# Decode-attention backward, 32 heads on one core: the second half of one head's dV stored as 124 and 4 partitions

## The chip, the cores and the metric

The kernel runs on one core of one Trainium2 chip. The core has five engines: TensorE for matrix products (PE; its weight loads are listed apart as PEld), VectorE (DVE), ScalarE (ACT), GpSimd (POOL) and SyncE (SP), which here only issues transfers. Besides them 16 DMA engines move data between the chip's memory (DRAM in the names) and the on-chip buffer SBUF, which has 128 partitions. A DMA instruction is issued by one engine's queue; it is cut into packets, each DMA engine moves its share in the order of issue, and each leaves a mark on a semaphore when its share has landed. The metric is device time in microseconds, from the program's start to its end; smaller is better.

## The reference

The reference runs softmax attention for 32 heads with one query row per head and 8192 keys of width 128 in bf16, and then its gradients for a given grad_out:

```
scores = einsum('bhqd,bhkd->bhqk', q, k) * scale
attn   = softmax(scores)
out    = einsum('bhqk,bhkd->bhqd', attn, v)
# and the vector-Jacobian product: dq, dk, dv
```

With p the attention row of a head and dO its grad_out row: dV = p (outer) dO, dP = V dO, dS = p * (dP - p.dP) * scale, dK = dS (outer) q and dQ = dS K. For each head two tensors of 2 MB are read (K, V) and two of 2 MB are written (dK, dV): 134.23 MB in and 134.23 MB out over the 32 heads.

## The kernel before

One loop over heads h from 0 to 32 (line 255 on) works on two heads at a time: the scores and dV of head h, and dK and dQ of head h - 1. The order of instructions on each engine is the order in which the code is written; the loop is a schedule made by hand.

A head's tensor lies in SBUF as 128 partitions of 64 rows of 128 values, so partition p holds rows 64p to 64p + 63, which is 16 KB that are contiguous in DRAM too. `load_k` (line 74) and `load_v` (line 78) issue one DMA of 2 MB each for a head; K has three buffers, V two. The gradients are made by `outer(h, which, r)` on VectorE: each call multiplies a quarter of the rows (r = 0 to 3; 128 x 2048 values, line 210) into a buffer `G_dk` or `G_dv`. Each of the two has two buffers, so head h needs the buffer that head h - 2 stored from.

`outer` also issues the store. Normally there is one DMA of 2 MB after r = 3 (`parts = 1`). For the first and the last head the store is cut in two halves along the rows of each partition (`parts = 2`): rows 0 to 31 of every partition after r = 1, rows 32 to 63 after r = 3. Each half has 128 partitions of 8 KB. All loads of K and V and all stores are issued on SP, in program order, and all of them go into one queue (q1). Towards the end that order is: load of V of head 31, dV of head 29, dK of head 29, dV of head 30, dK of head 30, dV of head 31 in two halves, the output row `out_0`, dK of head 31 in two halves, dQ. There are no loads after V of head 31. The small results `out_0` and dQ are 32 partitions of 256 bytes (line 253).

The semaphores that tell of landings are handed out in turn from eight, and a DMA waits until the one that used its semaphore last has landed. The dV of head 30 is stored from a buffer which no later head uses.

Of the kernel before, what the change touches and what calls it, by code (L numbers as in the profile page):

```python
# [23 lines left out]
def kernel(  # L24
# [11 lines left out]
    nc = tc.nc  # L36
    P = 128
    _, H, S, D = k.shape
# [23 lines left out]
    def rows_of(x, h, c, parts):  # L62
        L = NT // parts
        return x[0, h].rearrange("(p n) d -> p n d", p=P)[:, c * L:(c + 1) * L, :]

    def slots(X, c, parts):
        L = NT // parts
        return X[:, c * L:(c + 1) * L, :]
# [134 lines left out]
    def outer(h, which, r):  # L203
        x = st[h]
        if r == 0:
            x[which] = gpool.tile([P, NT, D], BF16, tag=which, name="G_" + which)
        G, dst = x[which], out_2 if which == "dk" else out_3
        rep, row = x["ds"] if which == "dk" else x["p"], x["qd"][:, 0 if which == "dk" else 1, :]
        Q = NT // 4
        nc.vector.tensor_tensor(  # L210
            slots(G, r, 4).rearrange("p n (a b) -> p n a b", b=R),
            slots(rep, r, 4).unsqueeze(2).to_broadcast([P, Q, D // R, R]),
            row.rearrange("p (a b) -> p a b", b=R).unsqueeze(1).to_broadcast([P, Q, D // R, R]),
            op=ALU.mult)
        parts = 1
        if h == 0 or h == H - 1:
            parts = 2
        if r % (4 // parts) == 4 // parts - 1:
            c = r // (4 // parts)
            nc.sync.dma_start(rows_of(dst, h, c, parts), slots(G, c, parts))  # L220

    def rows_bc(h):
        x = st[h]
# [31 lines left out]
    for h in range(H + 1):  # L255
# [9 lines left out]
        if h > 0:  # L265
            ds_of(p_)
            outer(p_, "dk", 0)
            dq_of(p_, 0)
# [3 lines left out]
        if h > 0:  # L272
            dq_of(p_, 1)
            outer(p_, "dk", 1)
# [9 lines left out]
        if h > 0:  # L284
            outer(p_, "dk", 2)
# [75 lines left out]
```

## Time and profile before

| what | value |
|---|---|
| median of 4 runs | 646.18 us (645.99 to 646.27) |
| the profiled execution | 646.26 us, of which 644.3 us span |
| DVE busy | 505.3 us (78%) |
| PE busy | 480.7 us (75%) |
| ACT busy | 183.6 us (28%) |
| moved by DMA | 269.80 MB, mean 419 GB/s over the span |
| mean granted TensorE clock | 0.599 |

The span goes from the first to the last instruction of the core; what lies around it in the profiled execution is 2.0 us. A busy share is an engine's own time at work. The strip of slices cuts the span in 40 equal parts of 16.1 us; its DMA row is the mean over the 16 DMA engines, in tenths, so that 8 can mean that all work for eight tenths of the time or that some have stopped. The queue table counts packets by queue: q1 carries what SP issues, q10 what ACT issues, and q8 and q14 fetch the engines' instructions. In the listing of instructions in order of time SPq stands for SP's sequencer: the moment a DMA is issued, not when it moves. In the table of waits each row is "who waited, for whom: us in total, times, longest". In the table of stretches the DMA share is again the mean over 16 engines, and 1.00 or a little more means that none of them rests.

### The profile page before, as it was taken

How to read it: one execution, taken by the hardware profiler on the slowest of the kernel's cores; microseconds unless marked ns; L12 is line 12 of the kernel's file. 1: busy time of each engine (PE TensorE's matmuls, PEld its weight loads, DVE VectorE, ACT ScalarE, POOL GpSimd, SP SyncE). 2: the span in 40 equal slices, each digit the busy share in tenths (PEclk: the TensorE clock that was granted, in tenths of full speed). 3: DMA queues.
4: the chain of work that ended last, by engine and by line, in shares of the span. 5: the costliest groups of instructions: out<-in, count | busy, mean ns of one | idle time of the engine just before them, and what ended most of it. 6: DMA issues, size and time to landing. Idle time of an engine off the chain costs nothing.

```text
span 644.3 us, 20935 instructions
## 1 busy us (share of the span) xinstructions
PE 480.7 (75%) x9673; PEld 451.7 (70%) x9673; DVE 505.3 (78%) x653; ACT 183.6 (28%) x332; POOL 0.7 (0%) x6
## 2 busy tenths in 40 slices
PE   2898888887677867778767787667786777877770
PEld 2888778886677866768666777667785676866670
DVE  5999898877977779777788777797767977778860
ACT  2333333232233221233222332223322223231230
POOL 0000000000000000000000000000000000000000
PEclk9666666665666655666656665556665666655665
DMA  8999999999999999999999999999999999999985
GB/s 349 405 426 429 426 421 430 425 428 429 427 429 426 428 428 425 432 424 431 427 426 429 427 428 429 427 426 425 430 426 426 427 429 427 427 430 426 428 367 241
DMA packets 19718, 269.80 MB, mean 419 GB/s; under 512 B 2352, under 2 KB 2352, under 8 KB 2864
## 3 DMA queue, kind: packets, MB, share of 16 engines
q1 hardware_dynamic: 19584, 268.47, 98.2%
q8 instruction: 75, 1.23, 0.7%
q14 instruction: 11, 0.09, 0.0%
q10 hardware_dynamic: 48, 0.01, 0.0%
HBM read 134.23 MB, written 134.23 MB: 417 GB/s over the span
## 4 chain that ended last, share of the span: by engine, by line
DMA 59%; PE 21%; DVE 14%; ACT 2%; issue 1%; SPq 0%; DVEq 0%; ACTq 0%
DMA Kt<-in_k_dram 48%; DVE XK_sb L146 8%; PE T_ps L183 8%; DMA out_dram<-G_dv 5%; DMA out_dram<-G_dk 5%; PE s_ps L157 5%; DVE G_dk L210 4%; PE dp_ps L200 3%; PE m_ps L200 2%; PE dp_ps L195 2%; ACT XT_sb L185 1%; PE m_ps L294 1%; DVE G_dv L210 1%; PE s_ps L173 1%; DVE sm L163 1%
## 5 line engine op out<-in xcount | busy, mean ns | idle before, releaser
L210 DVE TENSOR_TENSOR G_dv<-p_rep,qd 128x2048 bf16<-128x2048 bf16 x128 | 148.2, 1219 | 89.5 <-DMA out_dram<-G_dv 83.8
L183 PE MATMUL T_ps<-ident_f,Vt 128*128 128x128 f32 x1024 | 203.1, 382 | 0.2 <-PE m_ps L294 0.2
L183 PEld LDWEIGHTS T_ps<-ident_f,Vt 128*128 128x128 f32 x1024 | 190.5, 210 | 0.3 <-issue 0.2
L185 ACT COPY XT_sb<-T_ps 128x1024 f32<-128x1024 f32 x128 | 128.7, 1013 | 129.0 <-PE T_ps L183 126.9
L210 DVE TENSOR_TENSOR G_dk<-ds_rep,qd 128x2048 bf16<-128x2048 bf16 x128 | 155.6, 1218 | 2.4 <-DMA out_dram<-G_dk 1.4
L146 DVE STREAM_TRANSPOSE XK_sb<-Kt 128x1024 f32<-128x1024 f32 x128 | 148.2, 1213 | 5.9 <-DMA Kt<-in_k_dram 5.2
L157 PEld LDWEIGHTS <-XK_sb 128*128 128x128 bf16 x2048 | 57.6, 104 | 90.8 <-DVE pdt L234 79.8
L157 PE MATMUL s_ps<-q_blk,XK_sb 128*128 128x4 bf16 x2048 | 59.7, 168 | 82.2 <-DVE pdt L234 72.1
L195 PE MATMUL dp_ps<-do_blk,XT_sb 128*128 128x2 bf16 x2048 | 66.8, 164 | 17.9 <-ACT XT_sb L185 17.9
L195 PEld LDWEIGHTS <-XT_sb 128*128 128x128 bf16 x2048 | 65.1, 103 | 20.5 <-ACT XT_sb L185 20.5
L200 PE MATMUL dp_ps<-ds_rep,Kt 128*128 128x1 bf16 x2048 | 64.1, 165 | 1.6 <-issue 1.3
L200 PEld LDWEIGHTS <-Kt 128*128 128x128 bf16 x2048 | 59.6, 104 | 6.9 <-issue 6.8
L244 ACT COPY dq_all<-dp_ps 128x1 f32<-128x1 f32 x32 | 5.1, 159 | 192.3 <-PE dp_ps L200 185.4
L200 PEld LDWEIGHTS <-Vt 128*128 128x128 bf16 x2048 | 57.6, 97 | 1.0
L200 PE MATMUL m_ps<-p_rep,Vt 128*128 128x1 bf16 x2048 | 56.8, 164 | 0.0
L294 PEld LDWEIGHTS m_ps<-rs,ones_f 128*128 128x128 f32 x64 | 16.0, 311 | 49.9 <-ACT e L293 49.9
L294 PE MATMUL m_ps<-rs,ones_f 128*128 128x1 f32 x64 | 18.8, 362 | 40.5 <-ACT e L293 40.5
L303 ACT ACTIVATE p_rep<-e,rinv 128x256 bf16<-128x256 f32 x32 | 16.3, 509 | 30.0 <-DVE rinv L301 30.0
L163 DVE TENSOR_TENSOR sm<-s_ps,in_quad 128x256 f32<-128x256 f32 x32 | 13.6, 424 | 11.3 <-PE s_ps L157 8.2
L229 ACT CAST qd<-s_ps 128x256 bf16<-128x256 f32 x32 | 11.9, 372 | 32.2 <-PE s_ps L225 32.2
L236 DVE SCALAR_TENSOR_TENSOR ds_rep<-dp_ps,pdt,p_s 128x256 bf16<-128x256 f32 x32 | 15.5, 484 | 5.5 <-PE dp_ps L195 2.5
L293 ACT ACTIVATE e<-s_ps,nbias 128x64 f32<-128x64 f32 x32 | 10.0, 313 | 31.6 <-DVE nbias L290 31.6
(44 smaller groups left out, 143.3 us busy)
## 6 DMA issues: line engine op xcount, KB each, us to landing
Vt<-in_v_dram SPq DMA_DIRECT2D x32, 2048.0 KB, 30.0
Kt<-in_k_dram SPq DMA_DIRECT2D x31, 2048.0 KB, 30.8
out_dram<-G_dv SPq DMA_DIRECT2D x30, 2048.0 KB, 34.5
out_dram<-G_dk SPq DMA_DIRECT2D x30, 2048.0 KB, 33.6
out_dram<-G_dv SPq DMA_DIRECT2D x4, 1024.0 KB, 15.1
out_dram<-G_dk SPq DMA_DIRECT2D x4, 1024.0 KB, 13.5
Kt<-in_k_dram SPq DMA_DIRECT2D x4, 512.0 KB, 5.2
out_dram<-fin_sb SPq DMA_DIRECT2D x2, 8.0 KB, 13.4
```

Source lines behind the costliest of these rows:

```text
L146: nc.vector.transpose(XK[h][:, :, :, u, :], slots(Kt[h], u, NCH).rearrange("p g d -> p (g d)").bitcast(F32).rearrange("p (g w j) -> p g w ...
L157: nc.tensor.matmul(out[:, g, :], lhsT=cols[:, g, c // 2, c % 2], rhs=q_blk[:, h, c, :], start=(c == 0), stop=(c == 2 * NB - 1), skip_group ...
L163: nc.vector.tensor_tensor(x["sm"][:], x["s"][:, 0:NT].rearrange("p (a g) -> p a g", a=NQ).unsqueeze(2) .to_broadcast([P, NQ, NCH, CH]), in ...
L183: nc.tensor.transpose(T_ps[:, i, :], words[:, m * P:(m + 1) * P], ident_f[:])
L185: nc.scalar.copy(X[:], T_ps[:])
L195: nc.tensor.matmul(st[h]["dp"][:, n:n + 2], lhsT=X[:, i, e2, :], rhs=do_blk[:, h, e2, :], start=(e2 == 0), stop=(e2 == 1), skip_group_chec ...
L200: nc.tensor.matmul(out_col, lhsT=Xt[:, n, :], rhs=rep[:, n, 0:1], start=(n == 0), stop=(n == NT - 1), skip_group_check=True)
L210: nc.vector.tensor_tensor(slots(G, r, 4).rearrange("p n (a b) -> p n a b", b=R), slots(rep, r, 4).unsqueeze(2).to_broadcast([P, Q, D // R, ...
L229: nc.scalar.copy(x["qd"][:].rearrange("p a d -> p (a d)"), x["s"][:, 256:512])
L236: nc.vector.scalar_tensor_tensor(out=x["ds"][:], in0=x["dp"][:, 0:NT].unsqueeze(2).to_broadcast([P, NT, R]), scalar=pdt[:], in1=x["p_s"][: ...
L294: nc.tensor.matmul(x["m"][:, 0:1], lhsT=ones_f[:], rhs=rs[:], start=True, stop=True, skip_group_check=True)
L303: nc.scalar.activation(x["p"][:], e[:].unsqueeze(2).to_broadcast([P, NT, R]), ACT.Copy, scale=rinv[:])
```

## The change

For dV of head 30 (H - 2) the store is now cut in two halves as for the first and the last head. The first half goes out after r = 1 as 128 partitions. The second half goes out after r = 3 as two DMAs: partitions 0 to 123, and partitions 124 to 127. The bytes stored, their place in DRAM and all computation are the same; dK of head 30 is still one store.

```diff
         parts = 1
-        if h == 0 or h == H - 1:
+        if h == 0 or h == H - 1 or (h == H - 2 and which == "dv"):
             parts = 2
         if r % (4 // parts) == 4 // parts - 1:
             c = r // (4 // parts)
-            nc.sync.dma_start(rows_of(dst, h, c, parts), slots(G, c, parts))
+            if h == H - 2 and c == 1:
+
+                for lo, hi in ((0, P - 4), (P - 4, P)):
+                    nc.sync.dma_start(rows_of(dst, h, c, parts)[lo:hi], slots(G, c, parts)[lo:hi])
+            else:
+                nc.sync.dma_start(rows_of(dst, h, c, parts), slots(G, c, parts))
```

Described in a few words, the change is: second half of dV of head 30 stored as 124 and 4 partitions, so that these 1 MB move on DMA engines 0 to 3 alone.

## The prediction

> **What bounds the kernel now.** I read the strip of slices first, then the queues, then the stretches of the tail, the sync engine's issues, its waits, and last the single completion marks.
>
> ```profile
> span 644.3 us, 20935 instructions
> ...
> DMA  8999999999999999999999999999999999999985
> GB/s 349 405 426 429 426 421 430 425 428 429 427 429 426 428 428 425 432 424 431 427 426 429 427 428 429 427 426 425 430 426 426 427 429 427 427 430 426 428 367 241
> ...
> q1 hardware_dynamic: 19584, 268.47, 98.2%
> q8 instruction: 75, 1.23, 0.7%
> q14 instruction: 11, 0.09, 0.0%
> ```
>
> No compute engine is above 78% busy; the 16 DMA engines are at nine tenths or more from the second slice to the 38th, at about 428 GB/s. Transfers set the pace. Only the last two slices (8 and 5 tenths) have room. The second line to keep is q8: 75 packets that are no data of the kernel, but its instructions.
>
> ```profile
> core 0: us, PE busy (x) PEld busy (x) DVE busy (x) ACT busy (x) POOL busy (x), PEclk, DMA share, GB/s
> 560.00:600.00 40.00, 30.95 (x612) 29.16 (x610) 32.16 (x41) 11.31 (x21) 0.00 (x0) 0.57 1.01 428
> 600.00:610.00 10.00, 6.43 (x189) 5.96 (x185) 9.02 (x12) 1.54 (x3) 0.00 (x0) 0.60 1.02 431
> 610.00:620.00 10.00, 8.53 (x107) 7.92 (x108) 6.11 (x11) 3.91 (x7) 0.00 (x0) 0.54 0.89 377
> 620.00:630.00 10.00, 5.96 (x170) 5.50 (x167) 8.06 (x9) 2.37 (x8) 0.00 (x0) 0.63 0.90 377
> 630.00:633.00 3.00, 0.00 (x0) 0.00 (x0) 0.00 (x0) 0.00 (x0) 0.00 (x0) 0.50 0.96 404
> 633.00:640.00 7.00, 0.00 (x0) 0.00 (x0) 0.00 (x0) 0.00 (x0) 0.00 (x0) 0.50 0.57 240
> 640.00:643.00 3.00, 0.00 (x0) 0.00 (x0) 0.00 (x0) 0.00 (x0) 0.00 (x0) 0.50 0.18 72
> ```
>
> The DMA share falls to 0.57 and stays there for seven microseconds: 0.57 x 16 is nine engines at work and seven with nothing left. All computing has ended by 630.
>
> ```profile
> start us, us, engine line op out<-in xcount [idle before <-releaser]
> 593.76 0.33 SPq L220 DMA_DIRECT2D out_dram<-G_dk  x1
> 602.40 0.33 SPq L220 DMA_DIRECT2D out_dram<-G_dv  x1
> 614.01 0.33 SPq L220 DMA_DIRECT2D out_dram<-G_dk  x1
> 620.63 2.60 SPq L220 DMA_DIRECT2D out_dram<-G_dv  x2
> 624.76 0.33 SPq L253 DMA_DIRECT2D out_dram<-fin_sb  x1
> 627.18 2.60 SPq L220 DMA_DIRECT2D out_dram<-G_dk  x2
> 629.87 0.40 SPq L253 DMA_DIRECT2D out_dram<-fin_sb  x1
> ```
>
> ```profile
> engine line waited for: us in total, times, longest us
> ...
> SPq L356 <- DMA out_dram<-fin_sb: 12.9, 1, 12.9
> ```
>
> The store at 602.40 is dV of head 30, the one that changes. From the last issue the kernel waits 12.9 us for landings. Each DMA leaves one completion mark per engine in the trace; sorted, they part the engines in two groups:
>
> ```
> store            issued   five earliest   6th    7th    other nine
> dK head 29       593.76   607.8-608.0   609.1  612.9  620.8-623.0
> dV head 30       602.40   612.7-612.8   614.0  617.7  625.6-628.3
> dK head 30       614.01   620.1-620.2   620.3  622.5  630.4-633.2
> dV head 31, 1st  620.63   624.3-624.4   624.5  625.0  632.9-635.6
> dV head 31, 2nd  622.90   626.8-626.9   627.0  627.4  635.3-638.1
> dK head 31, 1st  627.18   630.9         631.0  631.1  637.8-640.6
> dK head 31, 2nd  629.45   633.4         633.5  633.5  640.2-643.0
> dq               629.87   633.5-633.6   633.6  633.7  640.4-643.2
> ```
>
> Nine engines lag by 13 to 15 us at dK of head 29. The lag grows over the whole run (at about 39 us every engine marks within 2.6 us), and the jumps fall where q8's packets do: the lagging engines fetch instructions as well. The end is the slowest of these nine, at 643.2; the others ran dry before 614.0, 620.6 and 627.2 while they waited for the next issue.
>
> **The change, part by part.** (1) dV of head 30 becomes three stores in place of one. The first half needs only two of the four products, which start at 597.74 and take 4.63 us, so it goes out near 600.1 and not 602.40. On a lagging engine it queues behind dK of head 29 (to 620.8 or later), on an early one behind the same store (to 607.8), so this is worth nothing: the backlog hides it. (2) Two more issues of 0.33 us on SP: SP is idle from 602.73 to 614.01, so nothing. What is queued behind them on SP is dK of head 30, which waits for its products until 614. Each new store also takes a completion semaphore last used eight DMAs back; the tightest of these waits is the last issue but one, which then needs the first half of dV of head 30: landed near 626, issued at 629.45 (dQ, issued at 629.87, needs the 124-partition store; late only under rival B). Nothing. No later head reuses this dV buffer, so nobody waits for the moved bytes either. DVE, PE and ACT instructions are the same, in the same order.
>
> (3) The bytes. One megabyte spread over 16 engines is 64 KB each; by the marks of the two halves of dV of head 31 (632.9 to 635.3, 635.6 to 638.1) an engine takes 2.45 us for it. By the description of the change these now lie on engines 0 to 3 alone: 256 KB each, 4 x 2.45 = 9.8 us. So twelve engines save 2.45 us, and four have 7.35 us more.
>
> If the four are early ones: their dK of head 29 ends at 607.9, the first half at 610.3, the moved megabyte at 620.1, dK of head 30 (4.9 us) at 625.0, and the four halves of head 31 at 634.8, each already issued by then. Before, their marks came 2.5, 1.9 and 1.6 us later than back-to-back work would have put them (612.7 to 620.1 for 4.9 us of work, 620.1 to 626.9, 626.9 to 633.4); these dry spells swallow 6.0 of the extra 7.35 us, and the four still end before the others. The nine have no dry spell, so their 2.45 us come off the end: 643.2 to 640.8. The next latest then is the same nine. The sum against the profiled execution: 646.26 - 2.45 = 643.8 us; the median of the four runs, 646.18, lies 0.08 under that execution, so 643.7 to 643.8.
>
> (4) The price that no row shows is that of a packet whose engine takes partitions which another engine is also emptying: every large DMA of before uses all 16 engines. The bound below is the usual one, 2.45 us for 64 KB. A gain beyond that I exclude, since stretches with everything busy never exceed it. Above, the nearest row is an instruction packet beside a data packet on one engine: 16 KB then take about 1.04 us in place of 0.61 in the packet list, 1.7 times; the longest 16 KB data packet, in the crowd at 27 us, took 1.95, 3.2 times. So 9.8 us lie between 9.8 and 31.4. I take 9.8: these are stores of plain 8 KB rows, and the 8 KB rows of head 31 keep pace beside engines that are busy elsewhere. The gain stays whole up to a factor of 1.6 (15.7 us, early end 640.7), is gone at 1.85, and at 3.2 the end is 656.4.
>
> [...]
>
> **Which engines are early** is the other thing that the views do not say. The packet list gives no engine numbers. Where an early and a late engine start packets in the same nanosecond and their sizes tell them apart (six separate pairings between 358 and 603 us), the early one is listed first; if the list goes by number, the early ones are the low ones. That leans to engines 0 to 3, no more. [...]
>
> **Rivals.**
> A, the forecast: 643.8 us, chance 0.53.
> B, the shared-partition price (slower): the four engines empty others' partitions at a factor over 1.6, and early engines become the last. End at 625.0 + 9.8 x factor; kernel 2.98 more: 646.2 at 1.85, 647.6 at 2, 652.5 at 2.5, 659.4 at 3.2. It decides from 1.85 on. For it: all 16 engines are at full pace between 603 and 612, and the nine never pause. Against: the slack of 6 us (634.8 against 640.8). Chance 0.30, of which 0.03 still gains, 0.06 is level and 0.21 slower.
> C, wrong engines: at least one of the four is among the nine. That engine ends 7.35 us later, at 647.8 to 650.6, kernel 650.7 to 653.5. For it: nine of sixteen lag. Against: the order in the packet list. Chance 0.11.
> D, the change does not confine the bytes: 124 partitions are spread like 128. Then only two issues are added, hidden by SP's idle 11 us: 646.2. For it: no row shows otherwise. Chance 0.06.
>
> **How the numbers follow.** Predicted: A, 643.8. A's own range is 643.3 to 644.6 (the lag of the nine differs by up to 2.8 us, and which of them fetches last may shift a little). The range to hold 8 in 10 must reach through C and most of B: 643.3 to 653.2, which leaves out B beyond a factor of 2.6 (about 0.11) and little else. 0.2% is 1.3 us, about what a measurement of this kernel can tell from no change. Faster: A and 0.03 of B, 0.56. Same: D and 0.06 of B, 0.12. Slower: C and 0.21 of B, 0.32.
>
> **What the changed profile would show.** Step 1 is right if the first half is issued near 600 and nothing else on SP moves. Step 3: the 124-partition store leaves four marks from transfers, near 620; dK of head 30 ends at 625 on four engines and before 631 on the nine; the share after 633 starts higher, as more engines are at work, and the end of landings is 640.8. Under B the four marks come after 626 and the last stretch is four engines alone; under C the moved store marks only near 633 to 636, and a few engines are alone at the end; under D sixteen marks up to 628. The forecast is wrong if the four engines are not early, or if rows from others' partitions cost more than 1.6 times the usual.

## The result, and the profile after

The changed kernel takes 647.3 us (median of 31 runs, 646.54 to 648.94); the kernel before, beside it, 646.28 us (median of 51 runs). The ratio is 1.0017, with a 95% interval of 1.0012 to 1.0022: slower by 1.0 us, where 2.45 us less was forecast. The profiled execution of the changed kernel took 648.94 us, 1.6 above its median, so the trace shows the loss larger than usual; the sum for it is made against 646.26, the profiled execution of before.

The page and the stretches of the tail, after (columns as before):

```profile
span 647.1 us, 20938 instructions
...
DMA  8999999999999999999999999999999999999995
GB/s 351 405 427 424 428 423 429 425 426 425 417 429 426 429 429 427 427 426 430 429 425 431 427 427 425 426 425 429 427 426 426 426 429 424 430 428 428 405 356 218
...
q1 hardware_dynamic: 19720, 268.47, 98.2%
q8 instruction: 75, 1.23, 0.7%
```

```profile
core 0: us, PE busy (x) PEld busy (x) DVE busy (x) ACT busy (x) POOL busy (x), PEclk, DMA share, GB/s
560.00:600.00 40.00, 30.89 (x613) 29.15 (x610) 32.50 (x42) 11.42 (x21) 0.00 (x0) 0.57 1.01 429
600.00:610.00 10.00, 6.86 (x208) 6.47 (x205) 8.46 (x10) 2.15 (x4) 0.00 (x0) 0.63 0.99 419
610.00:620.00 10.00, 7.85 (x87) 7.20 (x85) 6.24 (x11) 3.10 (x6) 0.00 (x0) 0.51 0.92 367
620.00:630.00 10.00, 7.04 (x205) 6.58 (x202) 8.59 (x10) 3.19 (x8) 0.00 (x0) 0.66 0.94 342
630.00:633.00 3.00, 0.00 (x0) 0.00 (x0) 0.39 (x1) 0.00 (x0) 0.00 (x0) 0.50 1.00 418
633.00:640.00 7.00, 0.00 (x0) 0.00 (x0) 0.00 (x0) 0.00 (x0) 0.00 (x0) 0.50 0.80 336
640.00:643.00 3.00, 0.00 (x0) 0.00 (x0) 0.00 (x0) 0.00 (x0) 0.00 (x0) 0.50 0.19 80
643.00:645.00 2.00, 0.00 (x0) 0.00 (x0) 0.00 (x0) 0.00 (x0) 0.00 (x0) 0.50 0.08 33
645.00:648.00 3.00, 0.00 (x0) 0.00 (x0) 0.00 (x0) 0.00 (x0) 0.00 (x0) 0.50 0.01 3
```

Read two columns together, the DMA share and GB/s. From 560 to 600 a share of 1.01 moves 429 GB/s. From 620 to 630 a share of 0.94 moves only 342: engines are busy, and their packets take longer. The share after 633 is 0.80 in place of 0.57, as forecast (the early engines have work), but from 643 to 645 it is 0.08, and 0.08 x 16 is one engine and a bit. A single engine sets the end.

SP issues the first half at 600.62 and the two cut pieces from 602.89, and waits for landings at the end:

```profile
start us, us, engine line op out<-in xcount [idle before <-releaser]
594.57 0.33 SPq L225 DMA_DIRECT2D out_dram<-G_dk  x1
600.62 0.33 SPq L225 DMA_DIRECT2D out_dram<-G_dv  x1
602.89 1.01 SPq L223 DMA_DIRECT2D out_dram<-G_dv  x2
615.06 0.36 SPq L225 DMA_DIRECT2D out_dram<-G_dk  x1
```

```profile
engine line waited for: us in total, times, longest us
SPq L361 <- DMA out_dram<-G_dk: 13.9, 1, 13.9
```

The completion marks tell whose end that is. The store of 124 partitions leaves one mark 0.4 us after its issue, which is no landing, and four at 623.7, 627.0, 628.7 and 630.9. So four engines do carry it, and they were to be done near 620. In the last half of dK of head 31 the sixteen marks are

```
three engines that were early and got nothing more   635.0, 635.0, 635.3
the nine late ones                                    639.4 to 641.0
the four that carried the megabyte                    638.7, 642.0, 643.7, 645.9
```

Each of the four ends 14.7 us after its own end of the moved bytes (one more row, then 4.9 us for dK of head 30 and four times 2.45 for head 31: 624.0, 627.3, 629.0 and 631.3 give 638.7, 642.0, 643.7 and 646.0). The nine lost their share of the megabyte and the last of them ends at 641.0, not 643.0; the gain is there. The four spent it. The marks carry no engine numbers; that these four belong to the same engines as the four marks of the 124 partitions is read from the equal distances.

In the packet list the moved rows take the usual 0.309 us until 615. Then 8 KB packets of 0.5 to 0.65 us are many, and about ten take 1.05 to 1.4 (from 621.6 on the halves of dV of head 31 are 8 KB packets too, and the list does not tell them apart). Of the 276 packets of 16 KB that start between 611 and 631, 259 take at most 0.65, where 0.611 is usual.

### The profile page after: what moved, and what is told of

The parts are those of the page before. It is cut to its first block, busy times and chain, and to the rows that moved or that the text cites. A ratio compares the mean times of both kernels' runs of the same rounds, so it can differ in the third digit from the quotient of the medians.

```text
span 647.1 us, 20938 instructions
## 1 busy us (share of the span) xinstructions
PE 479.5 (74%) x9673; PEld 450.7 (70%) x9673; DVE 505.3 (78%) x653; ACT 183.2 (28%) x332; POOL 0.7 (0%) x6
## 4 chain that ended last, share of the span: by engine, by line
DMA 59%; PE 21%; DVE 14%; ACT 2%; issue 1%; DVEq 0%; SPq 0%; ACTq 0%
DMA Kt<-in_k_dram 48%; DVE XK_sb L146 8%; PE T_ps L183 8%; DMA out_dram<-G_dk 5%; PE s_ps L157 5%; DMA Vt<-in_v_dram 5%; DVE G_dk L210 4%; PE dp_ps L200 3%; PE m_ps L200 2%; PE dp_ps L195 2%; ACT XT_sb L185 1%; PE m_ps L299 1%; DVE G_dv L210 1%; PE s_ps L173 1%; DVE sm L163 1%
```

## The experiments

Two theories to begin with. "Owner" supposes that every partition is emptied by one and the same engine in the stores of 128 partitions, its owner, and that a row taken by another engine is slow while that owner stores too. "Pair" supposes that each of the four engines takes 31 partitions in a row, and that two of them hinder each other when they take rows 31 apart at the same time, whatever the rest does. Both are the author's suppositions: no trace names the engine or the partition of a packet.

**The split alone.** Is it the four engines at all, or the halves?

```diff
-        if h == 0 or h == H - 1:
+        if h == 0 or h == H - 1 or (h == H - 2 and which == "dv"):
             parts = 2
```

> The kernel before with one part of the change alone: dV of head 30 in two halves of 128 partitions, no half on few engines. All theories agree: 646.2 us, within 0.5 of before, because the half that goes out 2.3 us earlier waits behind a backlog on every engine. If this alone is slower by 1 us, the whole loss of the change lies in the split and not in the four engines.

646.35 us (11 runs) against 646.31, ratio 0.9997 (0.9988 to 1.0006). As expected: nothing. All of the loss lies in what the four engines do.

**The cut store beside others, and alone.** Two stores of 124 partitions behind the end of the kernel before:

```diff
     result(dq_all, out_1)
+    for hh in (0, 1):
+        nc.sync.dma_start(rows_of(out_3, hh, 1, 2)[0:124], slots(st[H - 1]["dk"], 1, 2)[0:124])
```

> The kernel before plus two stores of 124 partitions x 8 KB behind the last one, one after the other, from the dK buffer of head 31 into the second halves of dV of heads 0 and 1, whose outputs are therefore wrong. The first runs from about 633.5 us beside nine engines that still store until 643, the second alone. No price at all: 31 rows x 0.306 = 9.5 us each, kernel 655.8. Theory 'owner' (a row is slow while the engine that usually empties its partitions stores too): the first takes about 13.7 us, the second 9.5 us with packets of 0.31 us; kernel about 660. [...]

660.01 us (one run). The first store ran from 633.6 and ended at 645.3, 646.6, 647.4 and 647.6 on its four engines, 11.7 to 14.0 us; the second took 9.5 to 9.7 us on each (654.8, 656.1, 657.1, 657.2). Stretches of that trace:

```profile
core 0: us, PE busy (x) PEld busy (x) DVE busy (x) ACT busy (x) POOL busy (x), PEclk, DMA share, GB/s
633.00:640.00 7.00, 0.00 (x0) 0.00 (x0) 0.00 (x0) 0.00 (x0) 0.00 (x0) 0.50 0.81 299
640.00:644.00 4.00, 0.00 (x0) 0.00 (x0) 0.00 (x0) 0.00 (x0) 0.00 (x0) 0.50 0.34 126
644.00:648.00 4.00, 0.00 (x0) 0.00 (x0) 0.00 (x0) 0.00 (x0) 0.00 (x0) 0.50 0.25 96
648.00:654.00 6.00, 0.00 (x0) 0.00 (x0) 0.00 (x0) 0.00 (x0) 0.00 (x0) 0.50 0.25 108
```

0.25 is four engines of sixteen. Alone they move 108 GB/s, 27 each, as each of the sixteen does when all are busy (429 from 560 to 600 after the change); beside nine others, 13 engines move 299, 23 each. The cut costs nothing by itself. "Pair" is not settled by this: the rows are the same in the second store, but its four engines begin it up to 2.3 us, some seven rows, apart, where the first store began on all four at once. A few rows at 0.4 to 0.6 us where the second store begins leave room for a little of it. The next two kernels have a price without any such pair.

**Own partitions or another engine's.** To part the owner from any store on four engines beside others: one store of four partitions, 16 KB a packet, twelve packets on each of four engines, behind the end. Once with partitions 0, 4, 8, 12, once with 64, 68, 72, 76. The author took the first for those that these four engines empty anyway, the second for those of four others. The trace names neither engines nor partitions, so this is an assumption, and what is said of owners below stands under it:

```diff
     result(dq_all, out_1)
+    NR = 12
+    nc.sync.dma_start(out_3[0, 0:NR].rearrange("h (p n) d -> p h (n d)", p=P)[0:16:4],
+                      st[H - 1]["dk"].rearrange("p n d -> p (n d)")[0:16:4].unsqueeze(1).to_broadcast([4, NR, NT * D]))
```

(in the second kernel `[64:80:4]` in both places)

> [...] Theory 'owner' (a row is slow only while the engine that usually empties its partitions stores too): full pace, 0.61 us a packet, four marks near 641.3, kernel 646.2. Theory 'few engines' (any store on four engines is slow beside others' stores, whatever its partitions): as slow as the moved megabyte, 1.2 to 1.5 times, marks at 642.5 to 645, kernel up to 648.

> [...] Theory 'owner': each of the four runs at about half pace while its owner still stores, to 640 to 643, then at full pace: marks at 643 to 645 for those with a late owner and near 641.3 for those whose owner is one of the early ones; kernel 646.5 to 648. Theory 'few engines': the same marks as with partitions 0 to 12.

Partitions 0 to 12: 645.97 us (one run), all four marks at 640.8. The stretches:

```profile
core 0: us, PE busy (x) PEld busy (x) DVE busy (x) ACT busy (x) POOL busy (x), PEclk, DMA share, GB/s
633.00:636.00 3.00, 0.00 (x0) 0.00 (x0) 0.00 (x0) 0.00 (x0) 0.00 (x0) 0.50 0.83 349
636.00:640.00 4.00, 0.00 (x0) 0.00 (x0) 0.00 (x0) 0.00 (x0) 0.00 (x0) 0.50 0.83 353
640.00:643.00 3.00, 0.00 (x0) 0.00 (x0) 0.00 (x0) 0.00 (x0) 0.00 (x0) 0.50 0.14 56
```

Partitions 64 to 76: 648.74 us (one run), marks at 641.0, 645.4, 645.4 and 645.9:

```profile
core 0: us, PE busy (x) PEld busy (x) DVE busy (x) ACT busy (x) POOL busy (x), PEclk, DMA share, GB/s
633.00:636.00 3.00, 0.00 (x0) 0.00 (x0) 0.00 (x0) 0.00 (x0) 0.00 (x0) 0.50 0.91 335
636.00:640.00 4.00, 0.00 (x0) 0.00 (x0) 0.00 (x0) 0.00 (x0) 0.00 (x0) 0.50 0.80 269
640.00:643.00 3.00, 0.00 (x0) 0.00 (x0) 0.00 (x0) 0.00 (x0) 0.00 (x0) 0.50 0.43 130
643.00:646.00 3.00, 0.00 (x0) 0.00 (x0) 0.00 (x0) 0.00 (x0) 0.00 (x0) 0.50 0.13 55
```

From 636 to 640 thirteen engines are busy in both (0.83 and 0.80), and move 353 or 269 GB/s. The packets say it most plainly: with partitions 0 to 12 all of them take 0.611 to 0.632 us; with 64 to 76 three engines' packets, after a first one of 0.91 to 1.03, take 1.19 to 1.28 us until the late engines end near 642, and from 642.6 on 0.611 to 0.62, while the fourth runs at 0.611 throughout. Under the assumption this fits three late owners and one early one, which had nothing left to store. It agrees with "owner": in this store 2.05 times the usual (1.25 over 0.611) while the late engines store, 1 otherwise. The two kernels differ in the place in DRAM as well, 1 MB further on in each head for the second; the fourth engine writes there too at full pace, which speaks against the place alone, but no run parts the two sides. The stores beside it pay as well, though later: from 637.1 on 8 KB packets of three engines take mostly 0.6 to 0.65 us in place of 0.309. The marks of the nine in the last half of dK of head 31 are 5.9 us later in sum than in the other kernel (640.0 to 643.2 against 640.0 to 642.9), three of them near 642.5 where 641 was usual.

**Seven engines in place of four.** If 119 = 7 x 17 partitions went to the seven early engines, each would carry only 17 to 19 rows. No trace shows engine numbers; 0 to 6 is the expectation's name for the seven.

```diff
-                for lo, hi in ((0, P - 4), (P - 4, P)):
+                for lo, hi in ((0, 119), (119, 126), (126, P)):
```

> The changed kernel with other cuts: the second half of dV of head 30 as 119, 7 and 2 partitions instead of 124 and 4, which should put 17 to 19 rows on each of seven engines (0 to 6) instead of 32 rows on each of four. If engines 0 to 6 are the seven early ones: the nine late ones still save 2.45 us, and the seven carry 5.2 to 5.8 us at full pace, at most 11.6 at half pace, which ends at or before 640.8 on each. Theories 'owner' and 'pair' both: 643.8 us. If one of engines 4 to 6 is late: 646 to 649.

652.03 us, ratio 1.009 (1.0077 to 1.0104): a miss. The seven marks of the 119 partitions are 616.4, 616.5, 617.3, 621.7, 630.7, 631.3 and 633.9. The first four of them lie about as far apart as four of the early marks in the trace before (607.9, 607.9, 609.1 and 612.9 at dK of head 29), so by these distances they are the four of the change again, and the three others are late engines. The store of two partitions marks at 617.1 and 618.0, in step with two of the three quickest. The issues show a second cost:

```profile
start us, us, engine line op out<-in xcount [idle before <-releaser]
620.31 2.60 SPq L225 DMA_DIRECT2D out_dram<-G_dv  x2
624.60 0.33 SPq L258 DMA_DIRECT2D out_dram<-fin_sb  x1
627.01 7.31 SPq L225 DMA_DIRECT2D out_dram<-G_dk  x2
```

```profile
engine line waited for: us in total, times, longest us
...
SPq L225 <- DMA out_dram<-G_dv: 7.7, 2, 6.6
```

The second half of dK of head 31 goes out at 634.0, not 629.4: it shares a semaphore with the store eight DMAs back, which with one DMA more is the 119 partitions, landed at 633.9.

**One head earlier.** The same cut in dV of head 29, so that, by "owner", more of the rows meet engines that load:

```diff
-        if h == 0 or h == H - 1 or (h == H - 2 and which == "dv"):
+        if h == 0 or h == H - 1 or (h == H - 3 and which == "dv"):
...
-            if h == H - 2 and c == 1:
+            if h == H - 3 and c == 1:
```

> The same cut of 124 and 4 partitions one head earlier, in dV of head 29: the four engines then reach the moved megabyte at about 600.5 (609 on the seventh earliest at most), while the late engines load V of head 31 for some 5 us of the 10. Theory 'owner': fewer rows meet a storing owner, so the four engines lose less than in the change, 1 to 4 us; the nine save 2.45 us; kernel 643.8 to 645. Theory 'pair': the slow rows do not depend on what the others do, so as slow as in the change, up to 20 us on the slowest of the four; but dV of head 31 waits for this buffer at 618, so products and issues are late by up to 5 us; kernel 646 to 649.

645.82 us, ratio 0.9997 (0.9988 to 1.0006): level, not faster. The price did fall. From the load of V of head 31 (600.4 to 600.8, 601.5 and 605.6 on the four) the megabyte took until 610.7, 612.2, 612.6 and 617.0: some 10 to 12 us, where 9.5 is usual and the change took about 13 to 17. That loading engines are the reason is not shown: by their marks the late engines stored until 608.1 to 611.4 and loaded V only from then on, so the cheaper rows, too, met late engines that stored for most of the time. What was gained went elsewhere: the first half of that dV now goes out at 580.42, ahead of the load of V of head 31 at 582.48. V landed at 616.7, not 613.2, and the last head's products and issues came 3 us later (dK of head 31 at 630.16, not 627.18). The expectation of 643.8 to 645 had not counted the load that the half was moved past.

**Fewer rows, in two places.** 92 = 4 x 23 partitions for four engines and 36 meant for twelve, first in dV of head 30, then in dK of head 29:

```diff
-                for lo, hi in ((0, P - 4), (P - 4, P)):
+                for lo, hi in ((0, 92), (92, P)):
```

> The changed kernel with the second half of dV of head 30 cut at 92 partitions instead of 124: 92 on four engines (23 rows each), 36 on twelve engines (3 rows each). The latest of the four was 5 us behind its fellows in the change and carried 32 rows at 1.47 times the usual; with 26 rows at that price it ends at 612.9 + 2.45 + 11.7 + 14.7 = 641.8, and at 1.3 times near 640.4. The nine late engines save 1.5 to 2.45 us: 641.7 at the latest. Theory 'owner' with the seventh engine as the limit: kernel 644.4 to 645.2, so faster than before by about 1.4 us. If the loss of the change came from the late engines themselves: no gain, 646 or more.

> The same cut at 92 in dK of head 29, one store earlier, dV of head 30 whole again: the four engines reach it at 605.5 (610.4 the latest of them), while the late ones load V of head 31 from 606.5 to 611.4. Theory 'owner': rows that meet an owner which loads cost nothing extra, so the price falls to 1.05 to 1.25 as in the run with dV of head 29; the four end before 639.5 and the nine at 641.7: kernel 644.4 to 645. If time makes no difference to the price: the same as the cut at 92 in dV of head 30.

646.65 us, ratio 1.0004 (0.9991 to 1.0018), and 646.71 us, 1.0014 (0.9999 to 1.0029): neither gains, both expectations missed in the time. The single runs spread from 645.1 to 650.3. The traces of one execution each (645.30 and 647.12 us) show who pays. The latest of the four took 11.5 us for 23 rows in dV of head 30 (7.0 at the usual pace) and 12.4 us in dK of head 29. The other three took 7.0 to 8.0 us in dV of head 30 and 7.0 to 7.9 in dK of head 29, the same, though by the marks the late engines stored for most of that time in the first kernel and loaded V for most of it in the second. So here the price does not follow what the late engines do; in both kernels it falls on the engine that reaches its rows last. Why these two kernels vary so much from run to run stays open.

**Half a megabyte, where the late engines load.** The first three quarters of a tensor as one store, the last as 124 and 4 partitions of 4 KB, in dK of head 29 (and, for the comparison, dV of head 30 with `h == H - 2 and which == "dv"`):

```diff
+        if h == H - 3 and which == "dk":
+            if r == 2:
+                nc.sync.dma_start(rows_of(dst, h, 0, 1)[:, 0:3 * Q, :], G[:, 0:3 * Q, :])
+            elif r == 3:
+                for lo, hi in ((0, P - 4), (P - 4, P)):
+                    nc.sync.dma_start(rows_of(dst, h, 3, 4)[lo:hi], slots(G, 3, 4)[lo:hi])
+            return
```

> The kernel before with a smaller and earlier move: of dK of head 29 three quarters go out as one store of 128 partitions after r = 2, and the last quarter (0.5 MB, rows of 4 KB) as 124 and 4 partitions. Each of the four engines carries 128 KB there, 4.9 us at full pace, and the twelve others save 1.22 us. Three of the four reach it at about 606.7, when the late engines load V of head 31 until 611.4: theory 'owner' gives them 4.9 to 5.5 us. The latest of the four starts near 611.6 beside storing owners and takes about 8.8 us, to end near 640; the nine then set the end at 642.0. Kernel 645.0 to 645.5, faster than before by 0.8 to 1.2 us. If the late engines lose what they save to the visitors: 646.2.

> The same half megabyte in the last quarter of dV of head 30, one store later. Theory 'owner': the four reach it near 611.6 (616.5 the latest), when the late engines store, so packets of 4 KB take up to twice 0.16 us for most of it: 8 to 10 us on each, the latest of the four ends at 639 to 641, still not after the nine at 642.0; but the late engines lose some 0.3 to 0.6 us to the visitors. Kernel 645.3 to 645.9. If the moment made no difference: the same as with dK of head 29.

In dK of head 29: 645.0 us (11 runs, 644.78 to 645.33) against 646.22, ratio 0.9979 (0.9970 to 0.9988). In dV of head 30: 645.41 us, ratio 0.9987 (0.9978 to 0.9996). The times of both are as expected, and the first beats the kernel before and the changed one; the intervals of the two overlap, so that the first place is better than the second is not clear of noise. The marks in the first are 610.8, 610.9, 612.4 and 616.6, so 4.8 to 5.2 us on each engine, almost the usual 4.9. In the second they are 615.9, 616.0, 617.4 and 623.3, so 4.5 to 6.2 us, where the expectation by "owner" had 8 to 10 on each: a miss in the mechanism. By the marks the late engines had loaded V of head 31 by 610.5 to 613.7 and stored dV of head 29 until 615.8 to 618.6, yet no 4 KB packet that starts before 619.3 takes over 0.173 us (0.159 is usual); only after that some of the latest engine's take about 0.31. That the late engines store is thus not enough for the price. Stretches of the first one's tail:

```profile
core 0: us, PE busy (x) PEld busy (x) DVE busy (x) ACT busy (x) POOL busy (x), PEclk, DMA share, GB/s
630.00:633.00 3.00, 0.00 (x0) 0.00 (x0) 0.00 (x0) 0.00 (x0) 0.00 (x0) 0.50 1.01 423
633.00:640.00 7.00, 0.00 (x0) 0.00 (x0) 0.00 (x0) 0.00 (x0) 0.00 (x0) 0.50 0.53 219
640.00:643.00 3.00, 0.00 (x0) 0.00 (x0) 0.00 (x0) 0.00 (x0) 0.00 (x0) 0.50 0.05 22
```

After 640 a share of 0.05 is left where before had 0.18; the last landing is at 642.2, 1.0 us sooner.

## Why the prediction was right or wrong

What held. The bound was read rightly: seven engines early, nine late, and the end set by the late ones. The first half sent out earlier is worth nothing (the split alone: ratio 0.9997). SP's two more issues were free: SP still waited 11.2 us before the next one (11.3 in the kernel before). The four engines are among the seven early ones, and the nine late engines end sooner, 639.4 to 641.0 in place of 640.2 to 643.0. From their marks of dK of head 29 (621.5 to 623.9, 0.7 later than before on average) to these they took 17.7 us on average in place of 19.7, so about 2.0 of the 2.45 us were saved on their side. Rival C (wrong engines) and rival D (not confined) are out.

What failed first is step 4, the price of the moved rows beside the other engines' stores. The prediction took 1.0, as "the 8 KB rows of head 31 keep pace beside engines that are busy elsewhere"; but those stores leave sixteen marks and the moved one four, so they were the wrong row to lean on. Measured, the two quickest to end of the four took 12.9 and about 16 us for 31 rows, the other two about 17 and 14.7, instead of 9.5, if the four keep their order: 1.4 to 1.8 times. In the cleanest case, with partitions 64 to 76, a packet cost 2.05 times while the late engines stored. This is rival B in size, a factor that can exceed 1.6. Its reason, that the four empty others' partitions, is not shown, as no trace names a packet's engine or partition; that those others must be storing agrees with that run and fails in dV of head 30 with half a megabyte. What the price depends on stays open.

A second term was mis-sized. Step 3 reckoned with four engines whose dK of head 29 ends at 607.9. Two of the four are the sixth and seventh of the seven, at 609.1 and 612.9 in the trace before, which stood in the same table of marks (with half a megabyte in dK of head 29 the third and fourth of the four marks come 1.5 and 5.7 us after the second). The seventh had 612.9 + 2.45 + 9.8 + 14.7 = 639.9, so it could bear a price of 1.1 and not of 1.6. In the profiled execution it reached dK of head 29 at 613.8; 613.8 + 2.45 + 14.7 + 14.7 = 645.7, where 14.7 is first its time for the moved rows and then the work behind them, and the last mark is at 645.9. So it is this engine that ends last, if the four keep their order. The "slack of 6 us" held for two of the four.

Both terms were needed. Rival B's formula starts from an engine that is free at 607.9: with 1.8, the dearest of the four, it gives 625.0 + 9.8 x 1.8 + 2.98 = 645.6, still a gain, against 647.3 measured. (At 1.85 and 3.2 that formula gives 646.1 and 659.3, not 646.2 and 659.4.)

What the runs show of the price and the spread: with partitions 64 to 76 three engines ran at about half pace (1.25 us for 0.611), but until 637.1 the 8 KB packets beside them kept 0.309 us, and with half a megabyte in dV of head 30 three engines paid nothing (no 4 KB packet before 619.3 took over 0.173 us). The store of 124 partitions, alone, ran at 27 GB/s on each of its four engines while some of them were rows apart; engines in step were not tested by themselves. The marks show how many engines carried a store, four for 124 partitions, seven for 119 and two for 2; that the four are numbers 0 to 3, as the description of the change says, they do not show.

## What to carry to other kernels

Before moving bytes from late engines to early ones, reckon with a price on the moved rows: here a packet on four engines beside other stores took between the usual time (0.611 us for 16 KB, partitions 0 to 12) and twice as much (1.25, partitions 64 to 76), and who was storing at that moment did not foretell it in every run. So measure the price where the move is to stand. Look up when each carrier comes free, and give the move a size that the slowest one can bear, not the average one: half a megabyte gained 0.1 and 0.2% in two places, a whole one lost 0.2%. And when a store is split, count the loads it now goes out ahead of (V of head 31 landed at 616.7, not 613.2) and the DMA eight issues later that shares its semaphore (issued at 634.0, not 629.4).

## What was not expected of the hardware

Nine of the sixteen DMA engines lag, by 13 to 15 us at dK of head 29, and the lag grows through the run (at about 39 us all sixteen marks of a DMA lie within 2.6 us), in which 75 instruction packets of about 1.0 us each come; by the distances of the marks three of the nine carried rows of the store of 119 partitions. In the change some 8 KB packets took 1.19 us, nearly four times 0.309; why is not shown. And the added store pays more than the stores beside it: in the run with partitions 64 to 76 three of its engines lost 4.4 to 4.9 us each (645.4 to 645.9 against 641.0) and the nine others 5.9 us together.
